# A two-layer transformer block on one core: P V as whole quads, a planner with new costs, ranks and rates, and no edited queues

## The chip, the cores and the metric

The kernel runs on one core of a Trainium2 chip. A core has five engines with queues of their own: TensorE (PE, matrix products), VectorE (DVE), ScalarE (ACT, functions such as exp and GELU), GpSimd (POOL) and SyncE (SP, here the issuer of DMAs). The metric is the device time of one execution in microseconds, as the median of several runs; lower is better.

## The reference

Two layers of the same four steps on x of 2048 rows (tokens) and 448 columns, in bf16:

```python
x = x + _A_ref(_layernorm(x), A_wqkv, A_wo)              # attention
x = x + _B_ref(_layernorm(x), B_w1, B_w2, B_w3, B_w4)    # mixer and MLP
# and both once more
```

`_A_ref` is attention without a mask: 16 heads of 28 columns, P = softmax(Q K^T / sqrt(28)), O = P V, then a product with wo. `_B_ref` normalises, multiplies by w1, takes GELU, shifts four groups of 112 columns by 1 or 2 rows up or down, multiplies by w2 and adds; then it normalises again, multiplies by w3 (448 to 1792), takes GELU, multiplies by w4 and adds. The GELU is the tanh form.

## The kernel before, in words

**Tiles.** Rows are cut into 16 tiles of 128. Queries go in chunks of 4, 4, 4, 2 and 2 tiles, heads in 4 groups of 4 (28 columns padded to 32, so that four heads share the 128 partitions). Scores are computed transposed: a *block* is 128 keys by 512 columns of (queries x key tiles) for one head, one PSUM bank. Each layer has 1024 blocks, 2048 in all.

**Exponentials.** `t_scores` (L1775) walks through the blocks and forms units of alternately three blocks (banks 0 to 2) and two blocks (banks 3 and 4). `t_exp` (L1877) takes each unit through one ScalarE instruction (L1892) into the tile PT. Some blocks go another way: `d_first` (L1734) reads the bank on DVE (L1736), and `d_chain` (L1747) makes 2 to that power by a polynomial in four more DVE instructions (L1763, L1765, L1767, L1770) into the tile PD. `ahead_of` (L1786) picks such blocks 6 to 13 key blocks ahead: for a free bank beside a unit by the table D_RATE, in place of a unit's third block by R_RATE. A rate is a ceiling on the share of a segment's blocks; it also needs a free buffer of each of two kinds (yd, PD), and a free bank. XSHUT says until when seven slots of V's tile serve as further buffers.

**P V.** `t_pv` (L1904) waits until two key blocks of all four heads are ready, and issues for each key tile four matmuls (a *quad*), one per head, each to 32 columns of the array (`tile_position`) and to 32 partitions of bank 5 (through `mm`, L1049 and L1050). Four such matmuls run side by side. The other products (L1059 in `mm4`) are cut into four column parts in the same way. Scores (L1654) use row parts of 32. In the plan these are two modes, "col4" and "r32"; a change of mode is charged.

**The planner.** All of this is Python that runs when the kernel is built. Each task is a generator that yields operations with an engine, a planned duration, and what they read and write. `Sched.run` (L618) takes the operation that can start first, by priority: the RANK table has one for each kind of work, layer and chunk (lower goes first). It adds TensorE fillers (`keep_pe_busy`, L557; the matmuls of L2385, products with an identity matrix that nobody reads) where TensorE would be idle. What comes out is one list of operations for each engine, in order; the waits on semaphores follow from what they read and write.

**Edited queues.** Behind the planner, `rearranged` (L274) moves single operations in the finished lists: MOVES has 370 pairs (an operation, and the one that it is put behind), WEAVE gives the order between engines in which they are entered again, and FILL_MORE repeats six fillers.

**GELU.** ScalarE has exp and GELU in different tables, and a change is an ACT_TABLE_LOAD. In the stream of exponentials a group's w3 results are copied to h2T by DVE (L2317) and take GELU in one instruction (L2339) when all are there. The mixer's GELU after w1 goes either of two ways: as a tanh, which the exp table also has, with products on DVE or POOL (L2156 to L2159), one for each of four column groups; or, for the chunks in PAIR, with a real GELU (L2140) in the same phase as the L2339 of a named group. After the last exponential ScalarE takes GELU straight from PSUM (L2313). TANHW names w3 groups that take the tanh way. `t_w4` (L2343) multiplies by w4, and `t_store` (L2367) adds and writes out (L2370).

Of the kernel before, what the change touches and what calls it, by code (L numbers as in the profile page):

```python
# [18 lines left out]
MOVES = (  # L19
# [46 lines left out]
)  # L66
WEAVE = (
    "vdvvvvsgdvgvvdtgtvgdtvtgdtsgtgvdvtvttdvtvvtdttvtvdgtgtdvtvtdtstvvtdgsvtttdtsgtttttstttsvttttvstgtttttttvtttttt",
# [707 lines left out]
RLO = 5  # L776
RHI = 7
RPRIO = 1
DWIN = 2
DTH = 0.4  # L780
XSHUT = (8, 83)
DLO = 6
# [1714 lines left out]
```

## Time and profile before

| what | us |
|---|---|
| median of three runs | 1024.03 (1023.98 to 1024.44) |
| span of the profiled execution, first to last instruction | 1022.4 |
| TensorE busy in it | 973.8 |
| ScalarE busy | 981.4 |
| VectorE busy | 811.0 |
| GpSimd busy | 292.3 |
| granted TensorE clock, mean | 1.000 |

The profile is of one execution. Busy times are unions of instruction times, so overlapping instructions are not counted twice in a sum by engine; a group's row gives the sum of its own instructions. A waiting instruction is not busy. "PE ps L1654" names the engine, the tile written and the line.

### The profile page before, as it was taken

How to read it: one execution, taken by the hardware profiler on the slowest of the kernel's cores; microseconds unless marked ns; L12 is line 12 of the kernel's file. 1: busy time of each engine (PE TensorE's matmuls, PEld its weight loads, DVE VectorE, ACT ScalarE, POOL GpSimd, SP SyncE). 2: the span in 40 equal slices, each digit the busy share in tenths (PEclk: the TensorE clock that was granted, in tenths of full speed). 3: DMA queues.
4: the chain of work that ended last, by engine and by line, in shares of the span. 5: the costliest groups of instructions: out<-in, count | busy, mean ns of one | idle time of the engine just before them, and what ended most of it. 6: DMA issues, size and time to landing. Idle time of an engine off the chain costs nothing.

```text
span 1022.4 us, 36170 instructions
## 1 busy us (share of the span) xinstructions
PE 973.8 (95%) x16283; PEld 412.9 (40%) x16285; DVE 811.0 (79%) x1572; ACT 981.4 (96%) x894; POOL 292.3 (29%) x462
## 2 busy tenths in 40 slices
PE   8999999999999999999999999999999999999998
PEld 4332443443433254333433443433433433454565
DVE  8777999989888958876877868688898589866651
ACT  8999999999999999999999999999999999999942
POOL 3312021531453016252325112012624120532230
PEclk9999999999999999999999999999999999999999
DMA  4643413320321013131131024423302020121101
GB/s 126 161 111 117 119 45 79 53 39 23 76 61 28 13 37 96 23 48 34 48 111 38 33 69 134 141 66 99 65 25 37 17 68 16 31 57 31 26 12 33
DMA packets 99394, 62.57 MB, mean 61 GB/s; under 512 B 68712, under 2 KB 88552, under 8 KB 99240
## 3 DMA queue, kind: packets, MB, share of 16 engines
q1 hardware_dynamic: 99240, 60.27, 23.6%
q8 instruction: 127, 2.08, 0.9%
q14 instruction: 27, 0.22, 0.1%
HBM read 28.16 MB, written 16.76 MB: 44 GB/s over the span
## 4 chain that ended last, share of the span: by engine, by line
ACT 71%; PE 23%; DVE 4%; DMA 1%; issue 1%; DVEq 0%
ACT PT L1892 65%; PE ps L1059 14%; PE ps L1654 5%; PE ps L1050 4%; ACT h2T L2339 2%; ACT fb L2158 1%; PE ps L2385 1%; ACT L1892 1%; DVE PD L1770 0%; ACT hT L2140 0%; DVE h2T L2317 0%; DMA xT<-xn 0%; ACT L2339 0%; DMA obf<-in_A_x_dram 0%; DVE yd L1736 0%
## 5 line engine op out<-in xcount | busy, mean ns | idle before, releaser
L1892 ACT ACTIVATE PT<-ps 128x1024 bf16<-128x1024 f32 (+1 forms) x782 | 887.3, 1333 | 2.9 <-PE ps L1654 2.1
L1654 PE MATMUL ps<-qT,kT 32*128 32x512 bf16 (+1 forms) x2304 | 269.8, 335 | 24.2 <-ACT PT L1892 18.4
L1050 PE MATMUL ps<-PT,vaug 128*32 128x512 bf16 (+1 forms) x2420 | 246.1, 341 | 0.7 <-ACT PT L1892 0.2
L1059 PE MATMUL ps<-xT,w 128*32 128x512 bf16 (+4 forms) x2656 | 177.9, 344 | 4.2 <-DVE h2T L2317 2.2
L1654 PEld LDWEIGHTS ps<-qT,kT 32*128 32x128 bf16 x2304 | 69.7, 91 | 256.0 <-ACT PT L1892 227.0
L2385 PE MATMUL ps<-ident 128*32 128x256 bf16 x3524 | 150.1, 276 | 1.8 <-POOL ident L1144 1.5
L2385 PEld LDWEIGHTS ps<-ident 128*32 128x32 bf16 x3524 | 98.9, 97 | 28.5 <-issue 11.9
L1050 PEld LDWEIGHTS ps<-PT,vaug 128*32 128x32 bf16 x2420 | 74.0, 95 | 89.4 <-issue 71.0
L1999 POOL TENSOR_TENSOR otn<-ub,fb 128x512 bf16<-128x512 f32 (+1 forms) x31 | 34.7, 1120 | 210.3 <-DMA fb<-rscr 202.9
L1736 DVE TENSOR_SCALAR yd<-ps 128x512 int32<-128x512 f32 x109 | 74.6, 685 | 22.8 <-PE ps L1654 21.7
L1059 PEld LDWEIGHTS ps<-xT,w 128*32 128x32 bf16 (+1 forms) x2656 | 69.2, 95 | 56.7 <-issue 25.0
L1763 DVE SCALAR_TENSOR_TENSOR fb<-yd 128x512 f32<-128x512 uint16 x109 | 78.5, 724 | 0.8
L1765 DVE SCALAR_TENSOR_TENSOR fb<-fb,yd 128x512 f32<-128x512 f32 x109 | 77.9, 717 | 0.7
L1770 DVE SCALAR_TENSOR_TENSOR PD<-yd,PD 128x512 int16<-128x512 int16 x109 | 75.9, 698 | 1.6
L1059 PE MATMUL ps<-w,h2T 128*32 128x448 bf16 x1120 | 75.4, 355 | 1.1 <-ACT h2T L2339 1.0
L2317 DVE CAST h2T<-ps 128x512 bf16<-128x512 f32 (+1 forms) x70 | 44.4, 635 | 16.2 <-PE ps L1059 15.0
L1392 POOL TENSOR_TENSOR sq<-qT 128x512 bf16<-128x512 bf16 x24 | 28.5, 1190 | 96.2 <-DVE qT L1451 93.4
L1392 POOL TENSOR_TENSOR sq<-kT 128x512 bf16<-128x512 bf16 (+2 forms) x32 | 30.4, 950 | 83.0 <-DVE kT L1406 79.9
L1767 DVE TENSOR_SCALAR PD<-fb 128x512 bf16<-128x512 f32 x109 | 49.6, 456 | 1.0
L1059 PE MATMUL ps<-xT,wk_pad 128*32 128x512 bf16 (+2 forms) x576 | 47.6, 359 | 0.7 <-DVE kT L1406 0.3
L1654 PE MATMUL ps<-wk_pad,kT 32*128 32x512 bf16 x256 | 39.6, 384 | 4.6 <-ACT PT L1892 4.0
L1059 PE MATMUL ps<-xT,wq_pad 128*32 128x512 bf16 x512 | 43.2, 382 | 0.5 <-issue 0.5
(189 smaller groups left out, 1195.9 us busy)
## 6 DMA issues: line engine op xcount, KB each, us to landing
uscr<-ub SPq DMA_DIRECT2D x28, 256.0 KB
ub<-uscr SPq DMA_DIRECT2D x28, 256.0 KB, 6.8
fb<-rscr SPq DMA_DIRECT2D x24, 256.0 KB
xnd<-xn SPq DMA_DIRECT2D x28, 128.0 KB, 2.3
xd<-x_res SPq DMA_DIRECT2D x16, 224.0 KB, 2.1
x_res<-xd SPq DMA_DIRECT2D x16, 224.0 KB, 4.2
w<-in_B_w_dram SPq DMA_DIRECT2D x5, 448.0 KB, 6.0
obf<-in_A_x_dram SPq DMA_DIRECT2D x16, 112.0 KB
```

The lines of the kernel that those rows point to most:

```text
L1050: return lambda e: e.matmul(out=out, lhsT=lhsT, rhs=rhs, start=start, stop=stop, **kw)
L1059: r.append(e.matmul(out=out[c:c + w, :], lhsT=lhsT[:, c:c + w], rhs=rhs, start=start, stop=stop, tile_position=(0, c)))
L1392: return both("sq", 0.15 + NW * 0.0018, 0.07 + NW * 0.00104, lambda e: e.tensor_tensor(out=sq[:, si, 0:NW], in0=src, in1=src, op=ALU.mult) ...
L1654: yield op("pe", (0.005 + NW * 0.00042) / nc_, lambda e, i=i, kc=kc, j=j, g=g, qt=qt, a=a, NW=NW, bank=bank: e.matmul(out=ps[:, bank, i * ...
L1736: yield op("dve", c_ps(512), lambda e: e.tensor_scalar(out=y, in0=ps[:, bi(bank), :], scalar1=SCALE * L2E * FS, scalar2=-126.0 * FS, op0=A ...
L1763: yield op(D_[0][0], D_[0][1], lambda e: e.scalar_tensor_tensor(out=q, in0=lo, scalar=E2 / E3 * FS, in1=lo, op0=ALU.add, op1=ALU.mult), re ...
L1765: yield op(D_[1][0], D_[1][1], lambda e: e.scalar_tensor_tensor(out=q, in0=q, scalar=E1 / E3 * FS * FS, in1=lo, op0=ALU.add, op1=ALU.mult) ...
L1767: yield op(D_[2][0], D_[2][1], lambda e: e.tensor_scalar(out=pdt, in0=q, scalar1=E3 / FS ** 3, scalar2=E0, op0=ALU.mult, op1=ALU.add), rea ...
L1770: yield op(D_[3][0], D_[3][1], lambda e: e.scalar_tensor_tensor(out=pdt.bitcast(I16), in0=hi, scalar=128.0, in1=pdt.bitcast(I16), op0=ALU. ...
L1892: yield op("act", 0.069 + n * w * 0.000833, lambda e, bk=bk, s0=s0, n=n, w=w: e.activation(out=PT[:, s0:s0 + n, 0:w], in_=ps[:, bk[0]:bk[0 ...
L2317: ev = op("dve", c_ps(m * NW), lambda e, hr=hr, pv=pv: e.tensor_copy(out=hr, in_=pv), reads=[("ps", bi(b))], writes=hk, touch=[b])
L2385: return [e.matmul(out=ps[32 * c:32 * c + 32, bi(b), 0:256].rearrange("p (a n) -> p a n", n=128), lhsT=ident[:, 32 * c:32 * c + 32], rhs=i ...
```

## The change

The planner and its tasks stay, and these things change:

- **Quads.** The four P V matmuls of a key tile are now one operation of the plan (`pv4`), which waits for the P of all four heads and which nothing can be planned into.
- **Planned durations.** The fixed part of an exponential goes from 0.069 to 0.054 us, that of a matmul operation from 0.008 to 0.0023, that of one P V matmul from 0.0015 to 0.0008, a filler from 0.12 to 0.11, a change of mode from 0.11 to 0.103. A filler now takes a bank only 1.59 us after the last ScalarE reader (0.2 before) and 0.83 us after a DVE reader (0.7).
- **Tables.** RANK, Q_LEAD, D_RATE, R_RATE, W_POS (when w3 and w4 are fetched), the priorities of the first tasks and the filler's window and target get other numbers. D_RATE has 59 entries (58), R_RATE 52 (61). XSHUT goes from (8, 83) to (10, 76), DHI from 13 to 12.
- **GELU pairs.** PAIR has one entry in place of three. PE_NORM and TANHW change for the last chunk of the second layer alone.
- **No edited queues.** MOVES, WEAVE and FILL_MORE are empty.

```diff
-MOVES = (
...
-WEAVE = (
...
-FILL_MORE = (
...
+MOVES = ()
+WEAVE = ()
+
+FILL_MORE = ()
...
-DWIN = 2
-DTH = 0.4
-XSHUT = (8, 83)
+DWIN = 1.714
+DTH = 0.403
+XSHUT = (10, 76)
 DLO = 6
-DHI = 13
+DHI = 12
 DPK = 2
-DDTH = 1.3
+DDTH = 1.502
...
-Sched.TARGET = 0.695
+Sched.TARGET = 0.833
...
-W_POS = (6, 9, 17, 5, 5, 5, 25, 21)
+W_POS = (12, 6, 16, 6, 5, 10, 33, 26)
...
-PAIR = {(0, 12): 7, (1, 4): 0, (1, 8): 3}
+PAIR = {(1, 4): 0}
...
+PVC = 0.0008
+MMC = 0.0023
+EXPC = 0.054
+FILLD = 0.11
+FMD = 0.83
+FMO = 1.59
+SWT = 0.103
...
+        def pv4(hs, vs, g, NW, i, start, stop):
+            def fn(e):
+                r = []
+                for j, (key, s) in enumerate(hs):
+                    buf = {"pd": PD, "pt": PT, "vaug": vaug}[key]
+                    r.append(e.matmul(out=ps[32 * j:32 * j + 32, 5, 0:NW], lhsT=vaug[:, vs, 32 * (4 * g + j):32 * (4 * g + j) + 32],
+                                      rhs=buf[:, s, i * NW:(i + 1) * NW], start=start, stop=stop, tile_position=(0, 32 * j)))
+                return r
+            return fn
...
-                            for j in range(4):
-                                key, s = home[(si, kb, j)]
-                                buf = {"pd": PD, "pt": PT, "vaug": vaug}[key]
-                                yield op("pe", max(0.018, 0.0015 + NW * 0.0001042), mm(ps[32 * j:32 * j + 32, 5, 0:NW], vaug[:, vs, 32 * (4 * g + j):32 * (4 * g + j) + 32],
-                                                                   buf[:, s, i * NW:(i + 1) * NW], done == 0, done == total - 1, tile_position=(0, 32 * j)),
-                                         reads=[("vaug", vs), (key, s)], writes=[(("ps", 5), j)], mode="col4", w=NW / 9600.0)
+                            hs = [home[(si, kb, j)] for j in range(4)]
+                            yield op("pe", 4 * max(0.018, PVC + NW * 0.0001042), pv4(hs, vs, g, NW, i, done == 0, done == total - 1),
+                                     reads=[("vaug", vs)] + hs, writes=[(("ps", 5), j) for j in range(4)], mode="col4", w=NW / 2400.0)
```

More of the change, by code (lines that the diff above doesn't have):

```diff
@@ L172 @@
-FILL_MORE = (
-    (2714, 4), (2725, 9), (3749, 15), (5548, 4), (5564, 4), (9810, 14),
-)
+MOVES = ()
+WEAVE = ()
+FILL_MORE = ()
 class _Op:
@@ L583, in keep_pe_busy @@
                 ds = self.P.deps("pe", reads, [key(b)])
-                if all(d.t_end + (0.7 if d.eng == "dve" else 0.2) <= t + 0.02 for d in ds.values()):
+                if all(d.t_end + (FMD if d.eng == "dve" else FMO) <= t + 0.02 for d in ds.values()):
                     pick = b
@@ L667, in run @@
                         if self.pe_mode is not None and self.pe_mode != m:
-                            start += 0.11
+                            start += SWT
                     elif eng == "act":
@@ L728, in run @@
                 m = kw.get("mode", "plain")
-                start = max(start, self.cur["pe"] + (0.11 if self.pe_mode not in (None, m) else 0.0))
+                start = max(start, self.cur["pe"] + (SWT if self.pe_mode not in (None, m) else 0.0))
                 self.pe_mode = m
@@ L771 @@
 PVB = 2
-DPRIO = 3.5
+DPRIO = 3.393
 DST = [('dve', 0.6), ('dve', 0.6), ('dve', 0.34), ('dve', 0.6)]
 DSEG = 1
-R_RATE = {0: 0.072, 1: 0.054, 2: 0.185, 3: 0.027, 4: 0.084, 5: 0.015, 6: 0.079, 7: 0.153, 8: 0.15, 9: 0.2, 10: 0.068, 11: 0.141, 13: 0.013, 14: 0.093, 15: 0.07, 16: 0.166, 17: 0.069, 18: 0.125, 19: 0.035, 20: 0.104, 21: 0.101, 22: 0.2, 24: 0.083, 25: 0.131, 26: 0.05, 27: 0.2, 28: 0.031, 29: 0.146, 30: 0.13, 31: 0.151, 32: 0.106, 34: 0.194, 35: 0.032, 36: 0.048, 37: 0.159, 38: 0.2, 39: 0.152, 40: 0.017, 41: 0.066, 42: 0.126, 43: 0.193, 44: 0.161, 45: 0.152, 46: 0.185, 47: 0.071, 48: 0.099, 49: 0.145, 50: 0.04, 51: 0.149, 52: 0.2, 53: 0.035, 54: 0.081, 55: 0.109, 56: 0.113, 57: 0.2, 58: 0.094, 59: 0.173, 60: 0.07, 61: 0.036, 62: 0.03, 63: 0.022}
+R_RATE = {2: 0.098, 3: 0.111, 5: 0.018, 6: 0.032, 13: 0.059, 20: 0.074, 22: 0.151, 25: 0.029, 29: 0.117, 31: 0.032, 32: 0.075, 35: 0.032, 37: 0.17, 38: 0.078, 39: 0.176, 41: 0.012, 42: 0.198, 43: 0.169, 44: 0.03, 45: 0.075, 46: 0.091, 54: 0.061, 56: 0.176, 59: 0.044, 62: 0.186, 33: 0.131, 63: 0.12, 16: 0.143, 23: 0.089, 18: 0.193, 27: 0.155, 61: 0.058, 49: 0.137, 30: 0.2, 53: 0.018, 0: 0.165, 40: 0.083, 8: 0.165, 1: 0.086, 26: 0.092, 48: 0.062, 60: 0.16, 55: 0.021, 52: 0.098, 4: 0.093, 9: 0.052, 15: 0.099, 10: 0.063, 28: 0.082, 7: 0.162, 47: 0.2, 12: 0.141}
 RLO = 5
@@ L789 @@
-Q_LEAD = {(0, 0): 0, (0, 1): 4, (0, 2): 45, (0, 3): 11, (1, 0): 18, (1, 1): 12, (1, 2): 4, (1, 3): 26}
-D_RATE = {1: 0.194, 3: 0.3, 4: 0.033, 6: 0.118, 7: 0.195, 8: 0.122, 9: 0.124, 10: 0.166, 11: 0.072, 12: 0.023, 13: 0.025, 14: 0.281, 15: 0.015, 16: 0.293, 17: 0.033, 18: 0.288, 19: 0.106, 20: 0.056, 21: 0.3, 22: 0.057, 23: 0.097, 24: 0.185, 25: 0.22, 26: 0.255, 27: 0.117, 28: 0.3, 29: 0.081, 30: 0.058, 32: 0.151, 33: 0.011, 34: 0.268, 35: 0.165, 37: 0.3, 38: 0.218, 39: 0.061, 40: 0.025, 41: 0.299, 42: 0.272, 43: 0.122, 44: 0.137, 45: 0.032, 46: 0.014, 47: 0.256, 48: 0.021, 49: 0.021, 50: 0.107, 51: 0.074, 52: 0.129, 54: 0.155, 55: 0.3, 56: 0.3, 57: 0.162, 58: 0.227, 59: 0.149, 60: 0.061, 61: 0.154, 62: 0.079, 63: 0.137}
@@ new lines @@
+Q_LEAD = {(0, 0): 0, (0, 1): 14, (0, 2): 46, (0, 3): 11, (1, 0): 18, (1, 1): 13, (1, 2): 55, (1, 3): 38}
+D_RATE = {1: 0.298, 6: 0.101, 7: 0.107, 8: 0.097, 9: 0.083, 10: 0.104, 11: 0.147, 12: 0.3, 13: 0.032, 14: 0.112, 15: 0.082, 16: 0.274, 18: 0.3, 22: 0.057, 24: 0.146, 25: 0.208, 26: 0.164, 27: 0.228, 28: 0.084, 29: 0.097, 30: 0.185, 32: 0.13, 33: 0.032, 34: 0.247, 35: 0.142, 37: 0.214, 38: 0.197, 40: 0.041, 41: 0.228, 43: 0.222, 44: 0.189, 45: 0.116, 46: 0.232, 47: 0.267, 48: 0.021, 50: 0.107, 51: 0.082, 52: 0.3, 54: 0.176, 55: 0.014, 56: 0.207, 57: 0.284, 58: 0.3, 59: 0.182, 61: 0.113, 63: 0.154, 4: 0.155, 5: 0.153, 53: 0.275, 19: 0.137, 36: 0.131, 17: 0.06, 0: 0.267, 21: 0.215, 49: 0.108, 23: 0.032, 2: 0.081, 3: 0.254, 42: 0.246}
@@ L793 @@
+PE_NORM = {(0, 0): 0, (0, 1): 0, (0, 2): 0, (0, 3): 0, (0, 4): 0, (1, 0): 0, (1, 1): 0, (1, 2): 0, (1, 3): 0, (1, 4): 3}
+TANHW = {(0, 0): 0, (0, 3): 0, (0, 7): 0, (0, 11): 1, (0, 13): 0, (1, 0): 0, (1, 3): 0, (1, 7): 0, (1, 11): 0, (1, 13): 1}
 Sched.AGED = 0
-Sched.TARGET = 0.695
+Sched.TARGET = 0.833
 Sched.LOW = 0
-Sched.WIN = 1.582
-Sched.LWIN = 3.6
+Sched.WIN = 1.943
+Sched.LWIN = 3.929
 GSL = 0
@@ L802 @@
 SMALL = [11, 12]
-W_POS = (6, 9, 17, 5, 5, 5, 25, 21)
-V_FIRST = 1.366
-K_FIRST = (0.756, 0.932, 1.363)
-Q_FIRST = (0.531, 1.956, 2.405)
+W_POS = (12, 6, 16, 6, 5, 10, 33, 26)
+V_FIRST = 1.89
+K_FIRST = (0.3, 0.453, 1.781)
+Q_FIRST = (0.308, 1.979, 3.146)
 Q_EARLY = 1
@@ L814 @@
 COLD = 6.0
-Sched.DOUBT2 = {"dma": 1.5, "pool": 0.2, "dve": 0.5, "act": 0.5, "pe": 0.0}
-Sched.EARLY = 0.1
-Sched.DOUBT = {"dma": 0.8, "pool": 0.6, "dve": 0.05, "act": 0.05}
+Sched.DOUBT2 = {'dma': 1.5, 'pool': 0.22, 'dve': 0.5, 'act': 0.49, 'pe': 0}
+Sched.EARLY = 0.099
+PVC = 0.0008
[5 more added lines that the diff above has]
+SWT = 0.103
+Sched.DOUBT = {'dma': 0.8, 'pool': 0.6, 'dve': 0.05, 'act': 0.05}
+Sched.LCRED = 0.3
 def PENORM(L, ch, g):
@@ L865, in c_mm @@
     def c_mm(n):
-        return 0.008 + n / 2400.0
+        return MMC + n / 2400.0
     def kc_of(L, t):
@@ L1891, in t_exp @@
                 w = max(128 * CHUNKS[segs[b_[0]][0]][segs[b_[0]][1]][1] * len(seg_kb[b_[0]][b_[1]]) for b_ in un)
-                yield op("act", 0.069 + n * w * 0.000833, lambda e, bk=bk, s0=s0, n=n, w=w: e.activation(out=PT[:, s0:s0 + n, 0:w], in_=ps[:, bk[0]:bk[0] + n, 0:w], func=ACT.Exp, scale=SCALE),
+                yield op("act", EXPC + n * w * 0.000833, lambda e, bk=bk, s0=s0, n=n, w=w: e.activation(out=PT[:, s0:s0 + n, 0:w], in_=ps[:, bk[0]:bk[0] + n, 0:w], func=ACT.Exp, scale=SCALE),
                          reads=[("ps", b) for b in bk], writes=[("pt", s0 + k) for k in range(n)], tab="exp")
@@ L2387, in filler @@
                     for c in range(4)]
-        SC.fill = (0.12, filler, ["b6", "b7", "b0", "b1", "b2", "b3", "b4"], lambda b: ("ps", bi(b)), [("ident",)])
+        SC.fill = (FILLD, filler, ["b6", "b7", "b0", "b1", "b2", "b3", "b4"], lambda b: ("ps", bi(b)), [("ident",)])
         SC.spawn(t_load(), 0)
```

110 lines of the change are left out of this document (2 added, 108 removed), and 46 rows, old and new, of the table MOVES.

## The prediction

> **What bounds the kernel now.** I read the page's engine totals first, then three stages cut at the first and the last exponential, then ScalarE's groups in the middle stage.
>
> ```profile
> span 1022.4 us, 36170 instructions
> ...
> PE 973.8 (95%) x16283; PEld 412.9 (40%) x16285; DVE 811.0 (79%) x1572; ACT 981.4 (96%) x894; POOL 292.3 (29%) x462
> ...
> ACT 71%; PE 23%; DVE 4%; DMA 1%; issue 1%; DVEq 0%
> ```
>
> ```profile
> 0.00:15.21 15.21, 12.71 (x239) 7.21 (x240) 11.47 (x51) 11.96 (x18) 5.32 (x18) 1.00 0.74 203
> 15.21:968.36 953.15, 909.97 (x14875) 373.26 (x14879) 780.12 (x1482) 949.25 (x846) 278.82 (x424) 1.00 0.25 61
> 968.36:1022.40 54.04, 51.09 (x1179) 32.46 (x1170) 19.41 (x39) 20.16 (x33) 8.19 (x20) 1.00 0.07 22
> ```
>
> The columns of the second fence are the stage, its length, and the busy time of PE, PEld, DVE, ACT, POOL. The head takes 15.21 us. In the stream, 953.15 us long, ScalarE is busy for 949.25 us: it is the bound there, and DVE has 173 us free. In the tail of 54.04 us ScalarE is busy for 20.16 us and TensorE for 51.09 us: TensorE is the bound there.
>
> ScalarE's work in the stream:
>
> ```profile
> L1892 ACT ACTIVATE PT<-ps 128x1536 bf16<-128x1536 f32 x375 | 582.8, 1554 | 2.2 <-PE ps L1654 1.5
> L1892 ACT ACTIVATE PT<-ps 128x1024 bf16<-128x1024 f32 x406 | 453.4, 1130 | 0.7 <-PE ps L1654 0.6
> L2339 ACT ACTIVATE h2T<-h2T 128x7168 bf16<-128x7168 bf16 x3 | 18.5, 6174 | 0.0
> L2158 ACT ACTIVATE fb<-fb 112x512 f32<-112x512 f32 x16 | 12.2, 788 | 0.7 <-DVE fb L2157 0.7
> ...
> L1892 ACT ACT_TABLE_LOAD x6 | 7.7, 1283 | 0.1
> ...
> L1892 ACT ACTIVATE PT<-ps 128x512 bf16<-128x512 f32 x1 | 0.6, 598 | 0.0
> ```
>
> ```profile
> 295.29 65.04 ACT PT L1892 x58
> ```
>
> The groups hold 375 x 3 + 406 x 2 + 1 = 1938 score blocks in 782 instructions. The two sizes differ by 424 ns, so a block of 512 elements costs about 0.4267 us. Neighbours overlap, so the fixed part must come from a stretch: the chain of waits has 58 exponentials in a row in 65.04 us. With 2.5 blocks each that is 61.87 us for elements and 3.17 us for the rest, 0.055 us per instruction. The whole work is then 1938 x 0.4267 + 782 x 0.055 = 870 us. The other ScalarE instructions of the stream sum to about 78 us in their rows. A row counts the overlap with the next instruction too (1554 ns for a step of 1.335 us, 0.22 us of overlap); for some 40 small ones that is 8 to 9 us, so they take some 70 us start to start. **What is left, 953 - 870 - 70, some 13 us, is all the stall of the stream.** The middle can thus get shorter by blocks taken off ScalarE far more than by fewer stalls.
>
> **The change, part by part.**
>
> *Fewer blocks on ScalarE (RANK, D_RATE, R_RATE).* There are 2048 blocks; the 110 that are not on ScalarE go through a chain on DVE:
>
> ```profile
> L1763 DVE SCALAR_TENSOR_TENSOR fb<-yd 128x512 f32<-128x512 uint16 x109 | 78.5, 724 | 0.8
> L1765 DVE SCALAR_TENSOR_TENSOR fb<-fb,yd 128x512 f32<-128x512 f32 x109 | 77.9, 717 | 0.7
> L1770 DVE SCALAR_TENSOR_TENSOR PD<-yd,PD 128x512 int16<-128x512 int16 x109 | 75.9, 698 | 1.6
> L1736 DVE TENSOR_SCALAR yd<-ps 128x512 int32<-128x512 f32 x109 | 74.6, 685 | 22.8 <-PE ps L1654 21.7
> L1767 DVE TENSOR_SCALAR PD<-fb 128x512 bf16<-128x512 f32 x109 | 49.6, 456 | 1.0
> ```
>
> One chain is 724 + 717 + 698 + 685 + 456 = 3.28 us of DVE. Units alternate three and two blocks, so 782 units should hold 391 threes; there are 375, which makes 16 blocks taken out of a three under R_RATE and 94 taken beside a unit under D_RATE. The D_RATE entries sum to 8.521 before and 9.517 after, the R_RATE entries to 6.584 and 5.362. Scaling the counts gives 105 and 13. A D block saves 0.4267 us and its share of an instruction, 0.4 x 0.055, together 0.449 us; an R block saves 0.427 us. So -11 x 0.449 + 3 x 0.427 = **-3.7 us**. The 8 more chains are 26 us of DVE, inside its 173 us free. Bounds: the rates are only ceilings, and free buffers decide as well, so 10 blocks fewer (+4.5 us) is possible; and 173 us hold 52 chains at most (-23 us). I take the value scaled by the rates, because it starts from the counted blocks.
>
> *P V of a key tile as one operation, planned durations as traced.*
>
> ```profile
> 301.31 0.39 PE L1654 MATMUL ps<-qT,kT 32*128 32x512 bf16 x3
> 301.63 0.40 PE L1050 MATMUL ps<-PT,vaug 128*32 128x512 bf16 x2
> 301.64 0.77 PE L1059 MATMUL ps<-w,hT 112*32 112x448 bf16 x8
> 302.34 0.39 PE L1654 MATMUL ps<-qT,kT 32*128 32x512 bf16 x2
> ```
>
> These are starts and lengths. Two of a quad's four P V matmuls go out at 301.63, and at 302.34 scores follow: the quad is parted. In the order that the kernel's lists give, scores stand inside some 230 of the 640 quads. A quad of 512 columns lasts about as long as one of its matmuls, so the second half is a further 0.2 us or so: up to 230 x 0.2 = 46 us of TensorE. It is less, since at 301.64, 10 ns after the half quad, a projection starts in the other columns. The Trainium skill, "TensorEngine Tiling (Array Packing)", section "Key Properties", says that tiles operate independently, and so that a half quad leaves no hole where other column work is at hand; by it the gain would be near nothing, and these two rows agree with it for this place. The plan's new costs fit the rows: scores to the next kind take 301.63 - 301.31 = 0.32 us, which is 512 columns and a switch of about 0.1 us (SWT was 0.11, is 0.103), and the exponential's fixed part, 0.055 us, is the new EXPC of 0.054 where the old one was 0.069. In the stream TensorE's freed time lies beside ScalarE, so by itself it saves nothing there; it makes scores late less often. The new operation waits for all four heads' P before its first matmul; behind it in TensorE's queue stand the scores of the next unit, for which ScalarE waits. The planner lets it go only when the whole batch is ready already, so I cost that wait at nothing; if it fails, it is paid in the next item.
>
> *No queue edits.* MOVES, WEAVE and FILL_MORE go: 370 moved operations in 197 chains, 117 of them on TensorE and 55 on DVE. What remains of stalls is 13 us now. A stall that an edit may have removed has the size of those that are left:
>
> ```profile
> 266.56 10.39 ACT L1892 ACTIVATE PT<-ps 128x1024 bf16<-128x1024 f32 x9 [0.60 <-PE ps L1654]
> 277.15 3.71 ACT L1892 ACTIVATE PT<-ps 128x1536 bf16<-128x1536 f32 x3 [0.20 <-PE ps L1654]
> ```
>
> At 0.20 us for each of the 117 + 55 chains the loss is at most 34 us. From below, better durations and whole quads could remove all 13 us. I take **+5 us**: a seventh of the upper end, since a plan in true durations makes by itself part of what the edits repaired.
>
> *GELU pairs.* PAIR keeps (1, 4) and loses (0, 12) and (1, 8). With the pair the chunk of tiles 8 to 11 of layer 1 waits for the GELU phase of group 3 to 6:
>
> ```profile
> 891.82 0.68 DVE L2128 TENSOR_SCALAR hT<-ps 112x512 bf16<-112x512 f32 x1
> ```
>
> ```profile
> 893.89 6.18 ACT L2339 ACTIVATE h2T<-h2T 128x7168 bf16<-128x7168 bf16 x1
> 899.97 1.90 ACT L2140 ACTIVATE hT<-hT 112x2048 bf16<-112x2048 bf16 x1
> ```
>
> ```profile
> 880.00:900.00 20.00, 8.44 (x276) 7.33 (x276) 1.00 0.12 30
> 900.00:920.00 20.00, 0.00 (x0) 0.00 (x0) 1.00 0.27 64
> ```
>
> ```profile
> 995.42 9.28 PE L1059 MATMUL ps<-xT,w 128*32 128x384 bf16 x224
> 1004.52 8.12 PE L1059 MATMUL ps<-w,PT 128*32 128x448 bf16 x168
> 1012.47 0.93 PE L1059 MATMUL ps<-w,kT 128*32 128x448 bf16 x16
> ...
> 1018.52 0.93 PE L1059 MATMUL ps<-w,kT 128*32 128x448 bf16 x16
> ```
>
> The last input is there at 892.5, but hT is ready at 901.9. Meanwhile TensorE runs 8.44 us of filler matmuls between 880 and 900 (L2385 alone, third fence), and after 900 none to the end: from there it has a backlog. It is this backlog that comes out at 1012.5, behind the last chunk's own work: 6.9 us of older w4 products to 1019.4. Without the pair each quarter goes its own way through DVE and a tanh of the exp table; about 3 us after 892.5 the chunk is ready, 6 us earlier, and the fillers' time is used. I take **-7 us** in the tail: these 6 us and 1 us from whole quads between 900 and 968. Bounds: nothing, if another wait holds the chunk; 15.3 us, if all 8.44 us and all 6.9 us go. The tanh way costs ScalarE 4 instructions in place of one, about **+0.5 us** with (0, 12), and DVE the products of L2156 to L2159, hidden in its free time; if that cover is gone, the chunk is late again and the 7 us are lost. W_POS, XSHUT, the first priorities and the filler settings move transfers and fillers on queues that are idle most of the time; I cost them at nothing, within 2 us.
>
> Sum: -3.7 + 5 - 7 + 0.5 = -5.2 us. The profiled execution has a span of 1022.4 us, and the median, 1024.03 us, lies 1.6 us above it. Span after 1017.2 us, time **1018.8 us**.
>
> **Rivals.**
>
> *Stalls take the place of edits* (slower). Planner order alone leaves ScalarE waiting for scores (L1654). For it: the 370 edits, and TensorE at 95% with little slack. Against it: the new costs match the rows. It decides from 12 us of new stalls, 61 of 0.20 us, a third of the chains. At half of them, 17 us: -3.7 + 17 - 7 + 0.5 = +6.8, **1030.8 us**. Chance 0.25.
>
> *A GELU phase moves into the stream.* If group 7 to 10 is done before the last exponential, its GELU runs there as one instruction (6.18 us) with two table loads (2 x 1.283), 8.7 us on the bound, where ScalarE now does it for nothing in the tail: -5.2 + 8.7, **1027.5 us**. For it: the earlier hT. Against: the tail loses that group's products. Chance 0.09. The Trainium skill, "ScalarE: Activation LUTs", section "What ACT_TABLE_LOAD costs", puts a switch at about 2.66 us with a drain; the estimate by it would be 2.8 us more, but the row has 1283 ns.
>
> *It does nothing*: buffers, not rates, set the DVE blocks, and another wait holds the last chunk: the terms cancel, **1024 us**. Chance 0.10.
>
> *Many more blocks on DVE*: 30 in place of 8, another 22 x 0.449 = 10 us off, **1009 us**. For it: 173 us of free DVE; against: the rates' sum. Chance 0.08.
>
> **How the numbers follow.** The forecast has a chance of 0.48, 1012 to 1022 us. With the last rival, faster by over 0.2% (2 us, about what a measurement can tell from no change) has 0.56, within it 0.10, slower 0.34. The range that holds 8 in 10 is 1006 to 1031 us; the forecast's own is 1012 to 1022.
>
> **What would show it.** L1736's successor counts some 118 chains and the exponentials some 1930 blocks; PE groups of P V come in whole fours; the stream is 949 to 956 us, the tail some 47 us with fillers gone before 900 or w4 of older groups no longer last. The stalls show as ScalarE's idle time before exponentials by scores. Wrong it would be if ScalarE's busy share in the stream fell below 98.5%, or if the stream got longer by a further GELU phase (more than the 6 table loads before exponentials, L1892).

## The result, and the profile after

The changed kernel takes **1029.13 us** (median of 4 runs, 1028.32 to 1029.74) against 1024.03 us (1023.98 to 1024.44): the ratio is 1.0047, with a 95% interval of 1.0033 to 1.0061. It is 5 us slower. The forecast was 1018.8 us, 5 us faster; the time lies inside the range that was given, but on the other side of no change.

From the page of the changed kernel, the span, the engine totals and the chain of work by engine:

```profile
span 1027.1 us, 38497 instructions
...
PE 973.3 (95%) x17443; PEld 414.8 (40%) x17445; DVE 823.3 (80%) x1587; ACT 980.3 (95%) x898; POOL 293.1 (29%) x462
...
ACT 83%; PE 13%; DVE 2%; DMA 2%; issue 0%; DVEq 0%; SPq 0%; ACTq 0%
```

The totals hardly moved; the chain that ended last runs through ScalarE for 83% of the span, where it was 71%. Cut again at the first and the last exponential (stage, length, busy time of PE, PEld, DVE, ACT, POOL):

```profile
0.00:17.06 17.06, 14.08 (x230) 8.05 (x231) 11.39 (x51) 11.89 (x17) 5.33 (x18) 1.00 0.63 181
17.06:972.86 955.80, 908.26 (x16039) 374.25 (x16036) 791.11 (x1496) 947.90 (x850) 280.61 (x425) 1.00 0.25 61
972.86:1027.10 54.24, 50.99 (x1190) 32.45 (x1178) 20.76 (x42) 20.50 (x33) 7.20 (x19) 1.00 0.08 24
```

Against before, the head is 1.85 us longer (17.06 for 15.21), the stream 2.65 us (955.80 for 953.15), and the tail 0.2 us (54.24 for 54.04). The stream's exponentials, by size:

```profile
L1748 ACT ACTIVATE PT<-ps 128x1536 bf16<-128x1536 f32 x378 | 614.1, 1625 | 6.5 <-PE ps L1510 6.4
L1748 ACT ACTIVATE PT<-ps 128x1024 bf16<-128x1024 f32 x403 | 477.8, 1201 | 0.8 <-PE ps L1510 0.8
```

378 x 3 + 403 x 2 = 1940 blocks, 2 more than before: VectorE took 108, not 118. The idle time before them is now 7.3 us, and 5.8 us of it is a single wait, in ScalarE's timeline (start, length, and the idle time before it):

```profile
540.53 1.05 ACT L1748 ACTIVATE PT<-ps 128x1024 bf16<-128x1024 f32 x1
547.41 2.36 ACT L1748 ACTIVATE PT<-ps 128x1536 bf16<-128x1536 f32 x2 [5.83 <-PE ps L1510]
```

TensorE's timeline of that place shows what ran ahead of the scores that ended this wait:

```profile
540.50 1.04 PE L915 MATMUL ps<-xT,wq_pad 128*32 128x512 bf16 x16
...
545.57 0.40 PE L915 MATMUL ps<-sq,astatq 128*32 128x512 bf16 x4 [0.56 <-DVE qT L1307]
...
546.98 0.39 PE L1510 MATMUL ps<-qT,kT 32*128 32x512 bf16 x4
```

This is the change of layers: layer 0's 1024 blocks are through at some 480 us, ScalarE is in layer 1, and the last mixers of layer 0 still run beside it. The query projection that starts at 540.50 is that of layer 1's second chunk (tiles 4 to 7); the first chunk had its own from 461.8 to 469.4 us. (The expectations of e6, e9 and e11 below call it layer 1's first.) At 540.5 ScalarE takes the last exponentials of the first chunk with key tiles 0 to 6, and the second chunk is next in the kernel's order. The statistic of the second chunk follows at 545.57 and its scores at 546.98. The view by tile, from 500 to 560 us, gives the first and last start of these projections, before and after:

```profile
L1059 PE MATMUL ps<-xT,wq_pad x64: 379/379/390, 527.4 to 537.5; 128*32 128x512 bf16 x64
```

```profile
L915 PE MATMUL ps<-xT,wq_pad x64: 379/379/390, 540.5 to 547.5; 128*32 128x512 bf16 x64
```

They are 13 us later, though ScalarE is only some 3 us behind (1131 blocks begun by 540.5 us, 1139 before). Their input is late. Tile 7 belongs to layer 0's group of tiles 7 to 10, and these are that group's residual additions (w4's products onto x_res), first and last start again:

```profile
L2355 DVE TENSOR_TENSOR x_res<-x_res,ps x4: 615/622/622, 505.0 to 523.7; 128x448 f32<-128x448 f32 x4
```

```profile
L2218 DVE TENSOR_TENSOR x_res<-x_res,ps x4: 620/622/622, 525.9 to 543.3; 128x448 f32<-128x448 f32 x4
```

The part that was meant to gain is there too. The P V row and the filler row of the page before, then of the page after:

```profile
L1050 PE MATMUL ps<-PT,vaug 128*32 128x512 bf16 (+1 forms) x2420 | 246.1, 341 | 0.7 <-ACT PT L1892 0.2
...
L2385 PE MATMUL ps<-ident 128*32 128x256 bf16 x3524 | 150.1, 276 | 1.8 <-POOL ident L1144 1.5
```

```profile
L1765 PE MATMUL ps<-PT,vaug 128*32 128x512 bf16 (+1 forms) x2423 | 202.7, 343 | 0.0
L2248 PE MATMUL ps<-ident 128*32 128x256 bf16 x4684 | 173.0, 276 | 1.8 <-POOL ident L1000 1.5
```

P V's row falls from 246.1 to 202.7 us; the planner issues 4684 filler matmuls in place of 3524, and TensorE's total stands still. (Rows of products that run side by side overlap, so they don't add up to the total.)

**A ledger.** For each kernel I took ScalarE's start times. The head ends at the first exponential. An exponential that waits for nothing is counted with 0.8333 ns per column and 53 ns (the commonest steps are 1331 ns for 1536 columns and 904 ns for 1024, which leaves 51 ns); what its step has beyond that is "late". "Other" is the rest of ScalarE's steps in the stream.

| kernel | median us | ratio to before | head | exps unstalled | late | other | tail | span |
|---|---|---|---|---|---|---|---|---|
| before | 1024.03 | 1 | 15.2 | 868.3 | 14.9 | 69.9 | 54.0 | 1022.4 |
| after | 1029.13 | 1.0047 | 17.1 | 869.1 | 16.3 | 70.4 | 54.2 | 1027.1 |
| before, unedited | 1028.46 | 1.0046 | 16.3 | 868.3 | 19.3 | 69.7 | 54.2 | 1027.8 |
| before, unedited, quads joined | 1023.81 | 0.9995 | 16.1 | 868.3 | 11.0 | 70.0 | 54.2 | 1019.6 |
| before, quads joined | 1020.48 | 0.9956 | 15.5 | 868.3 | 10.4 | 70.0 | 54.1 | 1018.3 |

The last three are experiments below. Of the 16.3 us late after, 6.0 us is the wait at the change of layers.

### The profile page after: what moved, and what is told of

Same layout as the page of the kernel before. It is cut to its first block, busy times and chain, and to the rows that moved or that the text cites. A ratio compares the mean times of both kernels' runs of the same rounds, so it can differ in the third digit from the quotient of the medians.

```text
span 1027.1 us, 38497 instructions
## 1 busy us (share of the span) xinstructions
PE 973.3 (95%) x17443; PEld 414.8 (40%) x17445; DVE 823.3 (80%) x1587; ACT 980.3 (95%) x898; POOL 293.1 (29%) x462
## 4 chain that ended last, share of the span: by engine, by line
ACT 83%; PE 13%; DVE 2%; DMA 2%; issue 0%; DVEq 0%; SPq 0%; ACTq 0%
ACT PT L1748 77%; PE ps L915 9%; ACT h2T L2202 2%; PE ps L1510 2%; ACT fb L2021 2%; PE ps L1765 1%; PE ps L2248 1%; ACT L1748 1%; ACT L2202 1%; DMA xT<-xnd 1%; DMA xT<-xn 0%; DMA xnd<-xn 0%; PE ps L1139 0%; ACT vaug L2202 0%; ACT sq L1245 0%
## 5 line engine op out<-in xcount | busy, mean ns | idle before, releaser
L1765 PE MATMUL ps<-PT,vaug 128*32 128x512 bf16 (+1 forms) x2423 | 202.7, 343 | 0.0
L2248 PE MATMUL ps<-ident 128*32 128x256 bf16 x4684 | 173.0, 276 | 1.8 <-POOL ident L1000 1.5
L915 PE MATMUL ps<-xT,w 128*32 128x512 bf16 (+3 forms) x2592 | 158.1, 341 | 3.2 <-DMA xT<-xn 1.5
L2248 PEld LDWEIGHTS ps<-ident 128*32 128x32 bf16 x4684 | 119.3, 98 | 38.8 <-issue 14.7
L1765 PEld LDWEIGHTS ps<-PT,vaug 128*32 128x32 bf16 x2423 | 58.9, 94 | 76.8 <-issue 68.6
L1592 DVE TENSOR_SCALAR yd<-ps 128x512 int32<-128x512 f32 x106 | 72.6, 686 | 17.2 <-PE ps L1510 16.2
L915 PEld LDWEIGHTS ps<-xT,w 128*32 128x32 bf16 (+1 forms) x2592 | 61.6, 95 | 55.3 <-issue 23.9
L915 PE MATMUL ps<-w,h2T 128*32 128x448 bf16 x1120 | 67.8, 354 | 1.0 <-ACT h2T L2202 0.6
L1623 DVE TENSOR_SCALAR PD<-fb 128x512 bf16<-128x512 f32 x107 | 46.8, 438 | 1.7
L2019 POOL TENSOR_TENSOR fb<-hT 112x512 f32<-112x512 bf16 (+1 forms) x21 | 23.8, 1133 | 63.3 <-DVE hT L1991 25.6
L1765 PE MATMUL ps<-PD,vaug 128*32 128x512 bf16 (+1 forms) x136 | 40.7, 339 | 0.0
```

What stands on the lines that cost most here:

```text
L915: r.append(e.matmul(out=out[c:c + w, :], lhsT=lhsT[:, c:c + w], rhs=rhs, start=start, stop=stop, tile_position=(0, c)))
L1592: yield op("dve", c_ps(512), lambda e: e.tensor_scalar(out=y, in0=ps[:, bi(bank), :], scalar1=SCALE * L2E * FS, scalar2=-126.0 * FS, op0=A ...
L1623: yield op(D_[2][0], D_[2][1], lambda e: e.tensor_scalar(out=pdt, in0=q, scalar1=E3 / FS ** 3, scalar2=E0, op0=ALU.mult, op1=ALU.add), rea ...
L1765: r.append(e.matmul(out=ps[32 * j:32 * j + 32, 5, 0:NW], lhsT=vaug[:, vs, 32 * (4 * g + j):32 * (4 * g + j) + 32], rhs=buf[:, s, i * NW:(i ...
L2248: return [e.matmul(out=ps[32 * c:32 * c + 32, bi(b), 0:256].rearrange("p (a n) -> p a n", n=128), lhsT=ident[:, 32 * c:32 * c + 32], rhs=i ...
```

## The experiments

The theory: the change is three things that nearly cancel, the lost edits (some 5 us slower), whole quads (some 5 us faster) and a new plan with a longer head and a wait at the change of layers (some 5 us slower). The rivals are the prediction's own terms: the block rates, the pair, quads that gain nothing.

**e1, the lost edits alone.** The kernel before with its three edit tables emptied.

```diff
-MOVES = (...)
-WEAVE = (...)
-FILL_MORE = (...)
+MOVES = ()
+WEAVE = ()
+FILL_MORE = ()
```

> The kernel before with MOVES, WEAVE and FILL_MORE empty and nothing else changed. Theory 1 (what is lost is the edits, and the new plan earns part of it back): over 1032 us, ScalarE's late exponentials in the stream sum to 22 us or more in place of 15. Rival (the edits were worth little, and the new plan is itself slower, by its own 6 us gap at the change of layers and its 2 us later head): 1024 to 1028 us, late exponentials 15 to 18 us.

1028.46 us (1027.37 to 1030.84), ratio 1.0046 (1.003 to 1.0062). The row of the three-block exponentials:

```profile
L1739 ACT ACTIVATE PT<-ps 128x1536 bf16<-128x1536 f32 x375 | 577.9, 1541 | 6.0 <-PE ps L1501 4.3 <-PE ps L897 0.8
```

Their idle time is 6.0 us where it was 2.2, and the ledger has 4.4 us more late and 1.1 us more head. The edits were worth 4.4 us, close to the +5 of the prediction, and not the 17 us of its rival. The result lies just above the range of this run's rival and far under theory 1. Among the edits are the 176 filler matmuls of FILL_MORE, and in this profile TensorE's granted clock is at half for 3.41 us from 703.5 us (0.57 on average from 703 to 707), where the profile before has no such stretch; the largest late step, 2.35 us, falls on it. How much of the 4.4 us is due to the clock, no run separates.

**e2, new costs on the old tables.** The changed kernel's new duration constants, with the old ranks, rates, pairs and window settings, and P V matmuls planned one by one as before.

```diff
-RANK, Q_LEAD, D_RATE, R_RATE, PAIR, ... as in the changed kernel
+RANK, Q_LEAD, D_RATE, R_RATE, PAIR, ... as before
...
-yield op("pe", 4 * max(0.018, PVC + NW * 0.0001042), pv4(...))
+for j in range(4): yield op("pe", max(0.018, PVC + NW * 0.0001042), mm(...))
```

> The changed kernel with all tables of before (ranks, rates, pairs, windows) and P V as four single operations; only the planned durations are new, and no edits. If true durations are what makes a plan good: at or below the changed kernel, 1022 to 1028 us. Rival (durations only rescale the plan's own clock): as slow as the unedited kernel before, within 3 us of e1, since the same queues come out in about the same order.

1037.84 us (1035.09 to 1040.07), ratio 1.0133 (1.011 to 1.0156), slower than the unedited kernel by 9 us.

```profile
L1748 ACT ACTIVATE PT<-ps 128x1536 bf16<-128x1536 f32 x376 | 573.7, 1526 | 10.2 <-PE ps L906 4.7 <-PE ps L1510 4.0
```

The idle time before these exponentials is 10.2 us. Both expectations missed. Durations nearer the trace do not make a better order by themselves: with tables that were set for other durations the order is worse.

**e3, whole quads undone in part.** The changed kernel with 188 of its quads parted in its final order, two matmuls left in their place and two put behind the next scores.

```diff
+        if held is None and o.pos in PARTED:
+            items.append((h, fa, ...))   # heads 0, 1
+            held = (h, fb_, ...)         # heads 2, 3, behind the next scores
```

> The changed kernel's queues as they are, but in 188 of the 640 quads the second two matmuls go behind the next scores. If a parted quad costs TensorE its full second half (0.216 us, 0.109 us for 256 columns): up to 30 us more TensorE time, ScalarE waits for scores and the kernel is 5 us or more slower. If half quads run beside other columns: within 2 us of the changed kernel, 1027 to 1031 us.

1037.49 us (1036.43 to 1038.75), ratio 1.0132 (1.0117 to 1.0147): 8.4 us over the changed kernel, 44 ns for each parted quad.

```profile
L1788 PE MATMUL ps<-PT,vaug 128*32 128x512 bf16 (+1 forms) x2423 | 271.3, 344 | 0.0
...
L2273 PE MATMUL ps<-ident 128*32 128x256 bf16 x4684 | 194.1, 276 | 1.6 <-POOL ident L1019 1.5
```

P V's busy time rises from 202.7 to 271.3 us with the same number of matmuls; TensorE's total rises from 973.3 to 996.9 us, 0.125 us a quad. A change of mode is not what costs it: in order of start, TensorE goes between scores and other matmuls 1524 times in both kernels.

**e4, the pair (1, 8) put back.**

```diff
-PAIR = {(1, 4): 0}
+PAIR = {(1, 4): 0, (1, 8): 3}
```

> The changed kernel with the pair (1, 8): 3 put back; the plan is the same up to the mixer of that chunk, at about 885 us. The prediction's step (the pair delays hT by 6 us and lengthens the tail by 7 us): hT some 10 us later than without, tail 60 us, 1034 to 1037 us. Rival (the tanh way is itself late, since its four ScalarE instructions wait behind the GELU phase too, and the pair costs nothing): hT ready earlier with the pair, tail within 2 us of 54 us, 1027 to 1031 us.

1032.46 us (1031.13 to 1033.76), ratio 1.0083 (1.0066 to 1.01): 3.3 us slower than the changed kernel. Its tail, and the GELU of the chunk of tiles 8 to 11:

```profile
970.80:1030.30 59.50, 56.15 (x1336) 35.77 (x1328) 28.04 (x58) 21.40 (x33) 11.66 (x26) 1.00 0.09 25
```

```profile
904.76 1.90 ACT L2003 ACTIVATE hT<-hT 112x2048 bf16<-112x2048 bf16 x1
```

With the pair that chunk is ready at 906.7, and without it at 913.0 (below). So the pair makes it earlier, the reverse of what the prediction had. The tail is longer all the same, 59.50 us: in this plan VectorE copies the w1 products of the last, 256-column chunk out of PSUM at 966.9 to 971.7, and in the changed kernel's at 946.8 to 951.6. So each expectation had half of it: hT as the rival said, the tail as the prediction's step said, but not by way of hT.

**e5, more fillers in the head.** One filler group of the changed kernel issued six times.

```diff
-FILL_MORE = ()
+FILL_MORE = ((69, 6),)
```

> The changed kernel with one of its head filler groups issued six times instead of once, twenty more filler matmuls in front of the first scores and nothing else. Theory (the changed kernel's head is 1.85 us longer than before because its plan puts 16 fillers instead of 21 ahead of the first transposes, TensorE then stands idle 1.54 us at 4.70 us and the granted clock stays at half until 10.7 us): the clock is full some us earlier, the head shrinks from 17.1 to between 15.2 and 16.3 us, and the median goes to 1027.3 to 1028.3 us. Rival (the half clock in the head does not follow the fillers, or the first exp waits for the input's transfers): head within 0.3 us of 17.1, median 1029 us. Second rival: the fillers stand in the way of the first transposes, head 18 us, 1030 us.

1027.49 us (1026.41 to 1029.56), ratio 1.0029 (1.0017 to 1.0041). The first exponential starts at 15.9 us instead of 17.06. TensorE between 5.5 and 10 us, in the changed kernel and then in this one (fillers, then transposes):

```profile
L2248 PE MATMUL ps<-ident 128*32 128x256 bf16 x36 | 2.1, 418 | 0.0
L1139 PE MATMUL ps<-ident,xn 128*128 128x128 bf16 x15 | 2.1, 307 | 1.1 <-DVE xn L1115 1.1
```

```profile
L2267 PE MATMUL ps<-ident 128*32 128x256 bf16 x72 | 2.5, 274 | 0.0
L1158 PE MATMUL ps<-ident,xn 128*128 128x128 bf16 x16 | 1.5, 220 | 0.7 <-DVE xn L1134 0.7
```

A filler takes 418 ns in the one and 274 ns in the other: in its profile the changed head runs on a slow TensorE, and this one does not. That the twenty fillers did it is not shown. e10 and e11 start with the changed kernel's own 64 filler matmuls, and their profiles have the fast TensorE and heads of 16.3 and 16.2 us; e1 starts with 84 and has the slow one (the rows stand in the last section). Against e10 and e11 the twenty fillers gain some 0.3 us of head. The median is 1.6 us under the changed kernel's, but the intervals of the two ratios overlap.

**e6, the second chunk's query projection earlier.** In the changed kernel's order, the projection of head group 0 and its statistic go ahead of the other three groups' and of a w4 product.

> The changed kernel with one edit of its queues at the change of layers: layer 1's first query projection and its statistic go ahead of the projections of the other three head groups and of a w4 product; nothing is added or left out. Theory (the 6.0 us stall of ScalarE at 541.6 us is the wait for that first projection, through its copy, square, statistic and scaling): the stall shrinks by 2.5 to 3 us, the stream ends as much earlier, and the median is 1026 to 1027 us. Rival (the scores that follow wait for something else at that point, keys or the other head groups): the stall moves a few hundred ns later and its sum stays, 1029 us.

1030.21 us (1029.44 to 1031.41), ratio 1.0052 (1.0039 to 1.0064): nothing gained. ScalarE's timeline:

```profile
544.39 2.37 ACT L1772 ACTIVATE PT<-ps 128x1536 bf16<-128x1536 f32 x2 [3.33 <-PE ps L1534]
549.23 1.45 ACT L1772 ACTIVATE PT<-ps 128x1536 bf16<-128x1536 f32 x1 [2.48 <-PE ps L1534]
```

The wait of 5.83 us became two of 3.33 and 2.48 us, 5.81 us in all. The theory falls, the rival holds: all four groups are late, since their input is, and ordering them among themselves only moves the wait.

**e7 and e8, whole quads on the kernel before.** Plan, tables, blocks and edits are those of before; in the final order the parted quads are brought together, in e7 at the place of their last part (228 quads), in e8 at the place of their first (226).

```diff
+        for quad in parted_quads:
+            # e7: quad[:3] go directly in front of quad[3]
+            # e8: quad[1:] go directly behind quad[0]
```

> The kernel before with all its queue edits, its plan and its blocks, in which 228 of the parted quads of P V matmuls are brought together by moving the first parts down to the last part. This is the change's first part alone on the old queues. Theory (each quad that other matmuls part costs TensorE time that the stream waits for, 45 ns each by the run that parts 188 quads of the changed kernel): 5 to 10 us faster, 1014 to 1019 us. Rival (where the old plan parted a quad TensorE had time to spare, and the late quads hold back the release of P tiles or the scores behind them): within 2 us of 1024. Second rival: the quads now stand as a block of 0.3 us in front of the next scores and these come late: 1026 to 1032 us.

> As the joined run beside it, but 226 of the parted quads of the kernel before are brought together by pulling the later parts up to the first one, so that the scores that stood between come behind the whole quad. Theory (cost of parting): 5 to 10 us faster, 1014 to 1019 us, as with the parts moved down. Rival (what counts is how early the scores are issued, not the parting): these scores are each up to 0.3 us later, many exps come late, slower than the other joined run by 3 us or more, and 1026 to 1035 us.

e7 takes **1020.48 us** (1020.0 to 1021.05), ratio 0.9956 (0.9943 to 0.9968): faster than both kernels. e8 takes 1063.75 us (1062.92 to 1064.01), ratio 1.0376 (1.0362 to 1.039). The page of e7 (totals, exponentials, P V), then the same two rows of the page of e8:

```profile
PE 946.6 (93%) x16283; PEld 385.5 (38%) x16285; DVE 809.1 (79%) x1572; ACT 978.6 (96%) x894; POOL 295.3 (29%) x462
...
L1908 ACT ACTIVATE PT<-ps 128x1024 bf16<-128x1024 f32 (+1 forms) x782 | 885.7, 1388 | 1.9 <-PE ps L1670 1.2
...
L1066 PE MATMUL ps<-PT,vaug 128*32 128x512 bf16 (+1 forms) x2420 | 200.7, 342 | 0.6 <-ACT PT L1908 0.2
```

```profile
L1908 ACT ACTIVATE PT<-ps 128x1024 bf16<-128x1024 f32 (+1 forms) x782 | 895.0, 1245 | 31.5 <-PE ps L1670 28.4
...
L1066 PE MATMUL ps<-PT,vaug 128*32 128x512 bf16 (+1 forms) x2420 | 236.2, 341 | 34.0 <-ACT PT L1908 32.3
```

e7 does the same 16283 matmuls in 946.6 us of TensorE instead of 973.8: 27.2 us less, 0.12 us a quad. Here too the changes between scores and other matmuls are the same but for two, 1516 for 1518. ScalarE gets 4.1 us of it (1024.58 us was the median of before beside these runs), less than the 5 to 10 us of the theory. In e8 the quads are whole in the queue as well, but TensorE stands 34.0 us in front of P V for exponentials that are not done, so that the four matmuls of a quad go out apart in time (TensorE is busy for 985.9 us, more than before); the next scores stand behind them, and ScalarE then waits 31.5 us for those. The slowdown is beyond what the rival had. A whole quad pays only where all four P are ready when it is issued.

**e9, whole quads without the edits.** The unedited kernel of e1 with its 244 parted quads joined as in e7: all of the change but the new plan.

> The kernel before without its queue edits and without its filler edits, in the order in which its old plan issues, with the 244 parted quads of that plan brought together by moving the first parts down to the last. It is the whole change except the new plan: no edits, whole quads, the old tables, blocks and pairs. Theory (whole quads are worth about 4 us whether the queues are edited or not, and the rest of the changed kernel's loss is its new plan with the late first projection of layer 1 and the longer head): 1024 to 1025 us, against 1028.5 us for the unedited kernel before, 4 to 5 us under the changed kernel. Rival (the new plan's whole quads are worth more than joined ones, and the plan is no worse): 1028 to 1030 us, the same as the changed kernel. Second rival (edits and joined quads remove the same late exps, so that without edits the quads bring more): 1020 to 1022 us.

1023.81 us (1021.3 to 1026.53 in 11 runs), ratio 0.9995 (0.9984 to 1.0006). This lies under the theory's 1024 to 1025 us by 0.2, and its profiled execution is at the fast end of its spread. Its stream:

```profile
16.09:965.38 949.29, 879.45 (x14710) 339.71 (x14710) 778.33 (x1482) 946.08 (x845) 281.05 (x424) 1.00 0.25 61
```

Joined quads took 4.65 us off e1's median (8.2 us off its span, all of it "late": 19.3 to 11.0). The new plan then puts 5.3 us on, against e9's median. This is net of TensorE's clock: e9's 11 runs have mean granted clocks of 0.993 to 0.998, where the changed kernel's four read 1.000, and in the profile it is at half for 3.41 us from 368.3 us. What that costs e9 no run separates.

**e10, the rates at their highest.**

```diff
-D_RATE = {1: 0.298, ...}
-R_RATE = {2: 0.098, ...}
+D_RATE = {i: 0.3 for i in range(64)}
+R_RATE = {i: 0.2 for i in range(64)}
```

> The changed kernel with both rates of VectorE blocks at the highest value that the tables hold, 0.3 and 0.2, for all segments, and nothing else; the plan is made anew from them. Theory of the prediction (the rates decide how many of the 2048 blocks VectorE takes, a unit of rate sum about 0.55 blocks): more than 150 blocks on VectorE and a stream some 15 us shorter, 1010 to 1015 us. Rival (buffers and score banks decide, the tables' sums do not): fewer than 120 blocks, and a plan with other waits, 1030 to 1055 us.

1056.54 us (1055.74 to 1058.21), ratio 1.0316 (1.03 to 1.0331), just above the rival's range.

```profile
L1748 ACT ACTIVATE PT<-ps 128x1024 bf16<-128x1024 f32 (+1 forms) x781 | 883.3, 1386 | 24.6 <-PE ps L1765 12.1 <-PE ps L1510 12.1
```

There are 373 exponentials of three blocks and 408 of two, 1935 blocks: VectorE gets 113, five more than in the changed kernel, from a rate sum more than twice as large. So the rates do not decide the number. By the kernel's code a block can also be refused for a buffer, a free bank, VectorE's load or keys that are not there yet; which of these it was, no run separates. The plan that comes out has 24.6 us of waits of ScalarE before exponentials, for 7.3 in the changed kernel.

**e11, the pair (0, 12) put back.**

```diff
-PAIR = {(1, 4): 0}
+PAIR = {(0, 12): 7, (1, 4): 0}
```

> The changed kernel with the GELU pair (0, 12): 7 put back, and nothing else; the plan is made anew from it. In the changed kernel the GELU phase of layer 0's group of tiles 7 to 10 starts at 514.7 us, in the kernel before at 491.4 us, and the first query projection of layer 1 at 540.5 instead of 527.4 us. Theory (the lost pair put that GELU phase back, and with it the first projection and the 6 us stall of ScalarE): with the pair the phase starts before 500 us, the stall falls under 2 us, and the median is 1024 to 1026 us. Rival (the new ranks and rates order the work of the layer change, the pair does not matter there): the phase comes some 5 us earlier, the stall keeps 5 to 6 us, and the median is 1029 to 1034 us.

1034.93 us (1033.75 to 1039.19), ratio 1.0113 (1.0087 to 1.014), just above the rival's range.

```profile
510.07 6.16 ACT L2202 ACTIVATE h2T<-h2T 128x7168 bf16<-128x7168 bf16 x1
```

```profile
544.57 4.62 ACT L1748 ACTIVATE PT<-ps 128x1536 bf16<-128x1536 f32 x4 [5.42 <-PE ps L1510]
```

The GELU of the w3 results of layer 0's tiles 7 to 10 comes 6 us earlier than in the changed kernel (516.0; before 493.7), the wait stays at 5.42 us. The pair is not its cause. The wait is in all profiles with the new ranks and rates (after, e3, e4, e5, e6 as two, e11) and in none with the old ones (before, e1, e2, e7, e8, e9). In e10, with the new ranks and other rates, the same group's residual additions run from 503.5 to 522.2 us, as early as before, and ScalarE still waits 4.31 us at about this place in the stream, there released by P V, which stands behind layer 1's V products in TensorE's queue. So the late group is not all that is wrong with the new order there, and no run takes the wait away. Which of the new entries put the group back stays open.

## Why the prediction was wrong

The forecast was 5.2 us faster. The two gains that made it, -3.7 and -7 us, did not come, and the order that the new plan gives, which no term priced, put 5.3 us on.

*Fewer blocks on ScalarE, -3.7 us.* **Failed.** It came out at 1940 blocks for 1938, +0.8 us of unstalled exponentials. The step scaled the counts by the sums of the rates; the text itself said that the rates are only ceilings, and e10 shows that the number of blocks hardly follows them. The rival "it does nothing" had this half right.

*GELU pairs, -7 us in the tail.* **Failed, with the sign of its mechanism.** The changed kernel, ScalarE and then DVE around the chunk of tiles 8 to 11 of layer 1:

```profile
890.59 1.28 ACT L2202 ACT_TABLE_LOAD   x1
891.88 6.18 ACT L2202 ACTIVATE h2T<-h2T 128x7168 bf16<-128x7168 bf16 x1
898.08 1.28 ACT L1748 ACT_TABLE_LOAD   x1
...
909.47 0.69 ACT L2021 ACTIVATE fb<-fb 112x512 f32<-112x512 f32 x1
```

```profile
896.24 0.69 DVE L1991 TENSOR_SCALAR hT<-ps 112x512 bf16<-112x512 f32 x1 [0.49 <-PE ps L915]
...
912.36 0.67 DVE L2022 SCALAR_TENSOR_TENSOR hT<-fb,hT 112x512 bf16<-112x512 f32 x1
```

The last input is there at 896.9, the last tanh runs at 909.47, and hT is done at 913.0: 16 us, where the step had 3. The four tanh stand behind the same GELU phase that the pair would have waited for, and then among the exponentials and DVE's other work. The chunk is 11 us later than before (901.9), not 6 us earlier. The tail did not move, 54.2 us for 54.0, since this chunk was not what it hung on; e4 says the same from the other side: the chunk 6 us earlier, the tail 5.3 us longer. That losing the pair is right in the new plan (3.3 us by e4) is luck as far as the step goes. The +0.5 us for the tanh way fits: "other" rose from 69.9 to 70.4 us.

*No queue edits, +5 us.* **Right in size**, +4.4 us by e1, but not by its reason: a plan in true durations was to make part of what the edits repaired, and e2, which has them on the old tables, is 9 us slower than e1. The rival of 17 us did not come; that its 1030.8 us lies near the result is luck.

*Whole quads, 1 us of the tail's term and else nothing.* **Mis-sized.** The joined runs give -4.1 and -4.65 us, and parting 188 quads costs 8.4 us. The upper bound of 0.2 us of TensorE a quad was sound (0.12 measured, three times). The error was to let it lie beside ScalarE: TensorE at 95% has little slack where scores are due, and less work in front of them makes them less late. The Trainium skill, "TensorEngine Tiling (Array Packing)", section "Key Properties", was read there as saying that a half quad leaves no hole. The measurement decides against that reading: with the same matmuls, in e7, TensorE loses 27.2 us. It is not the change of mode, whose number stays the same (1518 and 1516 in before and e7, 1524 in e1, e9, the changed kernel and e3); what is left, by elimination, is that some of the four column parts stand empty beside a half quad, and no run tests that alone.

*That the operation waits only when all is ready, nothing.* **Right**: the idle time before P V is 0.0 us in its row above. e8 shows the price where it isn't so.

*First priorities and filler settings, nothing within 2 us.* **Held for the head, at the edge**: it is 1.85 us longer in the profile. Some 0.8 us of that is the slow TensorE of this one execution, since e10 and e11 have the same first instructions and heads of 16.3 and 16.2 us; some 1.0 us is left for the plan.

*What no step had.* The new ranks and rates were costed only by the blocks that they move. **This is the step that is missing.** With the new plan layer 0's group of tiles 7 to 10 comes some 20 us later, and a wait of 6.0 us opens at the change of layers. It is the largest single piece of the loss. Along e1 and e9 the pieces are +4.4 us for the edits, -4.65 for whole quads and +5.3 for the new plan; as differences along one path they add up to 5.1 us by construction. The independent figure is e7's -4.1 us for whole quads.

The GELU phase did not move into the stream: six table loads each way, as before.

## What to carry to other kernels

When a planner's tables are replaced together with its costs, price the order that comes out of them, stage by stage, above all at hand-overs such as a change of layers; sums over a table say little when the table is a ceiling. And when one profile of a head is slow, compare it with other profiles of the same first instructions before naming a cause. Issuing the four matmuls of a quad together is worth something even where TensorE is not the bound, when the bound engine waits for what stands behind them, but only at the place where the last input is ready: the same grouping at the first part's place cost 39 us. Here the part worth keeping is the grouping on the old, edited order, 1020.48 us.

## What the runs showed of the hardware

A parted quad of P V matmuls cost TensorE 0.12 us in three pairs of runs (e3 against the changed kernel, e7 against before, e9 against e1: 23.6, 27.2 and 29.9 us over 188, 228 and 244 quads).

TensorE's speed in the head differs between profiles that start with the same instructions. TensorE's timeline, the changed kernel, e11 (the same first instructions) and e5:

```profile
1.52 3.61 PE L2248 MATMUL ps<-ident 128*32 128x256 bf16 x64 [1.52 <-POOL ident L1000]
6.24 1.03 PE L1139 MATMUL ps<-ident,xn 128*128 128x128 bf16 x8 [1.12 <-DVE xn L1115]
```

```profile
1.51 3.60 PE L2248 MATMUL ps<-ident 128*32 128x256 bf16 x64 [1.51 <-POOL ident L1000]
6.25 0.70 PE L1139 MATMUL ps<-ident,xn 128*128 128x128 bf16 x8 [1.14 <-DVE xn L1115]
```

```profile
1.51 4.13 PE L2267 MATMUL ps<-ident 128*32 128x256 bf16 x84 [1.51 <-POOL ident L1019]
6.30 0.70 PE L1158 MATMUL ps<-ident,xn 128*128 128x128 bf16 x8 [0.66 <-DVE xn L1134]
```

After 64 filler matmuls in 3.61 us and 1.12 us of idle time the eight transposes took 1.03 us; after the same fillers and 1.14 us, in e11, they took 0.70 us. With 64 fillers they took 1.03 or 1.04 us in five profiles (after, e2, e3, e4, e6) and 0.70 us in two (e10, e11); with 84 they took 0.70 us in four (before, e5, e8, e9), 0.88 us in e7 and 1.02 us in e1. So the number of fillers does not decide it alone.

The granted clock in the stage row reads 1.00 for all these heads, because time without a record counts as full. The trace's own records of the clock begin at full, at 10.71 us in the changed kernel, 5.53 us in e11 and 4.95 us in e5. The Trainium skill, "TensorE: Matmul & The Clock Gate", section "Part 1: The HAM clock gate (the "warmup" mystery)", says that the array runs at half rate until about one window of 3.4 us has been busy, and that this window runs freely. These profiles agree with it: count back from the first record by 3.41 us, the length of the half-clock stretches in e1 and e9. In e11 the window from 2.1 to 5.5 us holds 0.4 us of idle time. In the changed kernel the window from 7.3 to 10.7 us holds none, but the two ahead of it hold over 1 us each. In all twelve profiles that have such records (e7's has none) the window just ahead of the first record holds at most 0.42 us of idle time, and every earlier one that lies wholly in the span over 1.0 us. So, as far as these profiles go, where the window falls decides together with the fillers; a longer first stretch should make a busy window likelier, but no run here tests that.
